# A spectral block with an FFN on one core: the token transform put ahead of the model transform

## The chip, the cores and the metric

The kernel runs on one core of a Trainium2 chip. The core has TensorE (matmuls, PE; its weight loads are PEld), VectorE (DVE), ScalarE (ACT), GpSimd (POOL) and SyncE (SP, which here only issues DMAs), and 16 DMA engines. The metric is the time of one execution on the device, in microseconds; lower is better.

## The reference

x is 2048 tokens by 640 columns in bf16. From a vector c come six rows of 640 columns: mod = silu(c) @ w_mod, named sa, ca, ga, sb, cb, gb. Then:

```
h = layernorm(x) * (1 + ca) + sa
X = rfft2(h) over (tokens, columns)          # 2048 x 321 frequencies
x = x + ga * irfft2(X * (w_r + 1j * w_i))
h = layernorm(x) * (1 + cb) + sb
x = x + gb * ((silu(h @ w_gate) * (h @ w_up)) @ w_down)     # 640 -> 1728 -> 640
```

## The kernel before

Everything is one core's program, written out by hand: each engine runs its instructions in the order of the text, and the tile framework adds semaphores. Every DMA issued by SP stands in one queue in program order, and each also waits for the end of the eighth DMA before it.

**Layout of the tokens.** Partition p of row tile t holds token 16p + t, so there are 16 tiles of 128 x 640. The 640 columns are split as d = 4m + r, plus a last piece of 128 columns, and the 321 column frequencies are built from 81 (l = 0 to 80) by combining the four r.

**The forward stage** goes through the 16 tiles in the order SEQ. For a tile, t1 (L340, L341) transposes its five pieces on TensorE, and ACT copies them to SBUF as hT (L343). The mean and variance come for seven tiles (BN) from bn_stats on DVE (L348, L349), for the others from a Gram product on TensorE (gram_stats, L365) of which DVE sums the diagonal (L367); POOL takes the power -0.5 (L359). dfwd runs the model (column) transform with the table Rs, whose rows carry 1 + ca (dft_d, L320, L323). zout (L387, DVE) takes the mean out and writes Z. POOL scales the token table of this tile by the tile's standard deviation (gscale, L374, L375), and s1 (L398, L399) multiplies it with Z: a complex 128-point token transform, four matmuls of 324 columns. ACT writes the result to A_sb (L402; the last tile by pieces, L405), laid out as frequency l by (tile, re/im, r). The tables of seven tiles are mirror images of others, so those tiles are reversed in the copy of hT.

**The filter.** Wn holds w_i and w_r with a third part for their sum, 256 columns each. Wv holds the same for the mirrored token frequency: a DMA writes the reversed rows to DRAM (flip, L272, on SP; its first row by flip_edge, L266 and L268, on POOL), and another loads them back (L431). wsum (L412) adds w_r and w_i, on DVE or POOL, a range of l at a time.

**The spectral loop.** The 81 values of l are in 21 groups of four (48 to 63 first, then the edges 0 and 80, then 1 to 47, then 64 to 79). A_sb is transposed so that (tile, re/im, r) lies on partitions: the first groups on TensorE (t2_pe, L543, copies at L547 and L549), the rest by four DMA transposes (t2_dma, L524). The constant sa enters at token frequency 0 as a sum SA, added by POOL (L550, L564). Then, for a group: stage_a mixes the 16 tiles and the r by one matmul with KS2 (mix, L572) and DVE multiplies with the filter (prod, L599, twice); stage_b transposes the products back (L606) with a copy on ACT (L609); stage_c applies the inverse mix (L627), and evac writes E (L644; the edges L634 to L636). Since E is complex, rot writes a second, rotated copy (L655, on POOL or DVE). The matmuls with single columns of w_mod (mod_col, L585; mod_cols, L313) and ga (mod_bc, L660) are put in between.

**The inverse and the rest.** For each of 16 tiles s1em and s1er (L676, L685) run the inverse token transform from E with the table Htab, ACT copies (L680), the column transform with RI times ga follows (L1201, L1204), and DVE adds x and sums the row (L1206). From the fourth tile on, the second layernorm (L778 to L814, with a DMA transpose at L806) and the loads of the FFN weights (L751 to L763) run beside it. The FFN (L908, L931, L1018, L1030, L1060) goes in chunks of 2, 4, 4 and 6 tiles. L840 is a DMA that POOL issues to load and add FFN weights; the stores are at L901.

Of the kernel before, what the change touches and what calls it, by code (L numbers as in the profile page):

```python
# [23 lines left out]
NG9 = 9  # L24
BN = (0, 1, 4, 8, 10, 12, 14)
SEQ = (0, 1, 2, 15, 3, 14, 4, 13, 5, 12, 6, 11, 7, 10, 8, 9)
FLIP = (15, 14, 13, 12, 11, 10, 9)
# [8 lines left out]
def gslot(t):  # L36
    return t if t < NG9 else NT - t


def flipped(t):  # L40

    return t in FLIP


def _tables():

# [10 lines left out]
    T["R"] = R.astype(_NPBF)  # L67
    p = np.arange(P, dtype=np.float64)
    G = np.zeros((P, NG9, 2, 128))
    H = np.zeros((128, NT, 2, P))  # L70
    for t in range(NT):
        a = 2.0 * np.pi * ((p[None, :] * (16 * p[:, None] + t)) % S) / S
        if not flipped(t):
            G[:, gslot(t), 0, :] = -np.cos(a)
            G[:, gslot(t), 1, :] = np.sin(a)
        H[:, t, 0, :] = np.cos(a.T)
        H[:, t, 1, :] = np.sin(a.T)
    T["G"] = G.astype(_NPBF)
    T["H"] = H.astype(_NPBF)

    def real2(M):
        return np.array([[M.real, M.imag], [-M.imag, M.real]])

    q = np.arange(16)
    KS2 = np.zeros((16, 2, 4, 3, 2, 16, 2))
    KI = np.zeros((3, 2, 2, 16, 2, 16, 4, 2))
    for m in range(4):
        hl, mm = m // 2, m % 2
        k2 = q if hl == 0 else 15 - q
        F16 = np.exp(-2j * np.pi * np.outer(q, k2) / 16)  # L90
        for r in range(4):
            M = real2(F16 * (-1j) ** (m * r))
            if hl:
                M[:, 1] *= -1
            M = M.transpose(2, 0, 1, 3)
            KS2[:, :, r, 1, hl, :, mm] = M[:, :, 0]
            KS2[:, :, r, 0, hl, :, mm] = -M[:, :, 0] - M[:, :, 1]
            KS2[:, :, r, 2, hl, :, mm] = M[:, :, 1] - M[:, :, 0]
            f = (1.0, 1j ** r, (-1.0) ** r, (-1j) ** r)[m]
            for v in range(3):  # L100
                M = real2(F16.conj().T * f * (np.exp(1j * np.pi * r / 4) if v == 2 else 1.0))
                if hl:
                    M[1] *= -1
                if v >= 1:
                    M[:, 1] *= -1
                KI[v, hl, :, :, mm, :, r, :] = M.transpose(0, 2, 3, 1)
    K = np.zeros((128, 3 * 128 + 192))
    for v in range(3):
        K[:, 128 * v:128 * v + 128] = KI[v].transpose(1, 0, 2, 3, 4, 5, 6).reshape(128, 128)
    K[:, 384:] = KS2.reshape(128, 192)  # L110
    T["K"] = K.astype(_NPBF)
# [45 lines left out]
def adaln_block_kernel(ctx, tc, A_x, A_w_r, A_w_i, B_x, B_w_gate, B_w_up, B_w_down, c, w_mod, out):  # L157
# [3 lines left out]
    G_dram = nc.inline_tensor(T["G"], name="tab_G").ap()  # L161
    H_dram = nc.inline_tensor(T["H"], name="tab_H").ap()
    K_dram = nc.inline_tensor(T["K"], name="tab_K").ap()
    RI_dram = nc.inline_tensor(T["RI"], name="tab_RI").ap()

    x_v = A_x.rearrange("o (p t) d -> p (o t) d", t=NT)
    out_v = out.rearrange("o (p t) d -> p (o t) d", t=NT)
# [16 lines left out]
    KS2 = Ktab[:, 384:576]  # L184
# [10 lines left out]
    ssq = const.tile([P, NT], F32, name="ssq")  # L195
    mv = const.tile([P, NT, 2], F32, name="mv")
    bn6a = const.tile([P, 2, 6], F32, name="bn6a")
    rstd = const.tile([P, NT], F32, name="rstd")
    mhalf = const.tile([P, 6], F32, name="mhalf")
    vtmp = const.tile([P, NT], F32, name="vtmp")  # L200
    sc_f = const.tile([P, NC5], F32, name="sc_f")
# [6 lines left out]
    SAx = gb_bc[:, 0:512].rearrange("p (l k) -> p l k", l=4)  # L208
# [4 lines left out]
    wm_sa = rM.cut(6400, [NC5, D])  # L213
    wm_r = rM.cut(12800, [NC5, 4, D])
    A_sb = rA.cut(0, [NL, NT, 2, 4])
    Wn = rW.cut(0, [3, NT, NW])
    Wv = rW.cut(24576, [3, NT, NW])
    Htab = rH.cut(0, [NT, 2, 128])
    RI = rH.cut(8192, [2, 4, 160])
    o = 0  # L220
    Gtab = rE.cut(o, [NG9, 2, 128]); o += 8192
    Rp = rE.cut(o, [5, RC]); o += 1620
    Rs = rE.cut(o, [2, 4, RC]); o += 2592
    Cb = rE.cut(o, [4, 162], F32); o += 2592
    oHT = o; o += 1300 * 5
    oZ = o; o += 1296 * 4
    oGS = o; o += 768 * 4
    oSQ = o; o += 256

    SL = rY.cut(3072, [5, 2, 128])  # L230
# [13 lines left out]

    nc.scalar.dma_start(c_row[:], c)
    wmca_v = wm_v[:, :, D:2 * D]
    nc.sync.dma_start(x_sb[:, 0:1, :], x_v[:, 0:1, :])
    nc.sync.dma_start(wm_ca[:, 0:3], wmca_v[:, 0:3])
    nc.scalar.dma_start(Rp[:, 4:5], R_dram[:, 4:5])
    nc.sync.dma_start(wm_ca[:, 3:5], wmca_v[:, 3:5])  # L250
    nc.sync.dma_start(Rp[:, 0:4], R_dram[:, 0:4])
    nc.sync.dma_start(x_sb[:, 1:2, :], x_v[:, 1:2, :])
    nc.sync.dma_start(x_sb[:, 2:3, :], x_v[:, 2:3, :])
    nc.sync.dma_start(x_sb[:, 15:16, :], x_v[:, 15:16, :])
    nc.sync.dma_start(Gtab[:, 0:4], G_dram[:, 0:4])
    nc.sync.dma_start(x_sb[:, 3:5, :], x_v[:, 3:5, :])
    nc.sync.dma_start(x_sb[:, 13:15, :], x_v[:, 13:15, :])
    nc.sync.dma_start(x_sb[:, 5:7, :], x_v[:, 5:7, :])
    nc.sync.dma_start(Gtab[:, 4:NG9], G_dram[:, 4:NG9])

    dram = ctx.enter_context(tc.tile_pool(name="dram", bufs=1, space=bass.MemoryType.DRAM))
    Wflip = [dram.tile([P, NT, NW], BF16, name=n) for n in ("wflip_i", "wflip_r")]

    def flip_edge(w, f):
        ncol = w.ap[0][0]
        nc.gpsimd.dma_start(f[0:1, 0:NT - 1, :], bass.AP(tensor=w.tensor, offset=w.offset + P * ncol + 65,  # L266
                                                        ap=[[P * NT * ncol, 1], [P * ncol, NT - 1], [1, NW]]))
        nc.gpsimd.dma_start(f[0:1, NT - 1, :], w[0:1, 65:65 + NW])  # L268

    def flip(w, f):  # L270
        ncol = w.ap[0][0]
        nc.sync.dma_start(f[1:P].rearrange("p k l -> k p l"),  # L272
                          bass.AP(tensor=w.tensor, offset=w.offset + 127 * ncol + 65,
                                  ap=[[P * ncol, NT], [-ncol, P - 1], [1, NW]]))

    nc.sync.dma_start(x_sb[:, 10:13, :], x_v[:, 10:13, :])
    flip(A_w_i, Wflip[0])
    nc.sync.dma_start(x_sb[:, 7:10, :], x_v[:, 7:10, :])
    flip(A_w_r, Wflip[1])
    nc.sync.dma_start(wm_sa[:], wm_v[:, :, 0:D])  # L280
    for i, w in ((0, A_w_i), (2, A_w_r)):
        nc.sync.dma_start(Wn[:, i, :, :], w.rearrange("(k2 k1) l -> k1 k2 l", k1=P)[:, :, 0:NW])
    wm_m = wm_v[:, :, 2 * D:6 * D].rearrange("p k (i d) -> p k i d", i=4)
    nc.sync.dma_start(wm_r[:, :, 0, :], wm_m[:, :, 0, :])
    nc.sync.dma_start(KS2, K_dram[:, 384:576])
# [6 lines left out]
    for i in range(5):  # L292
        nc.vector.memset(rE.cut(oHT + 1300 * i, [NC5, 130])[:, :, 128:129], 1.0)
    nc.gpsimd.memset(identb[:], 0.0)
    nc.gpsimd.affine_select(out=identb[:], in_=identb[:], compare_op=ALU.not_equal, fill=1.0, base=0,
                            pattern=[[-1, 128]], channel_multiplier=1)
    nc.scalar.activation(warm[:], warm[:], ACT.Silu)
# [18 lines left out]
    def dft_d(zps, lhs, R):  # L316
        M = lhs[0].shape[-1]
        for h in range(2):
            o_all = zps[0:M, h, 0:2 * RC]
            nc.tensor.matmul(o_all, lhsT=lhs[4], rhs=R[:, 1, 2 * h:2 * h + 2, :].rearrange("p r n -> p (r n)"),  # L320
                             start=True, stop=False)
            for rr in range(2):
                nc.tensor.matmul(zps[0:M, h, rr * RC:(rr + 1) * RC], lhsT=lhs[2 * h + rr], rhs=R[:, 0, 2 * h + rr, :],  # L323
                                 start=False, stop=(rr == 1))

    def zview(zps, M=P):
        return zps[0:M, :, 0:324]


    if True:  # L330
        t1b, hTs, Zs, Gss = {}, {}, {}, {}

        def zbank(t):
            return banks(2 + 2 * (t % 2), 2, [2, 512])

        def t1(t):
            xt = banks(t % 2, 1, [NC5, 128], BF16)
            xr = x_sb[:, SEQ[t], 0:512].rearrange("p (m r) -> p r m", r=4)
            for r in range(4):
                nc.tensor.transpose(xt[:, r, :], xr[:, r, :], identb[:])  # L340
            nc.tensor.transpose(xt[:, 4, :], x_sb[:, SEQ[t], 512:640], identb[:])  # L341
            hT = rE.cut(oHT + 1300 * (t % 5), [NC5, 130])
            nc.scalar.copy(hT[:, :, 0:128], _rev(xt, 127, [[128, NC5], [-1, 128]]) if flipped(SEQ[t]) else xt)  # L343
            hTs[t] = hT

        def bn(t):
            for k in range(2):
                nc.vector.bn_stats(bn6a[:, k, :], x_sb[:, SEQ[t], 320 * k:320 * k + 320])  # L348
            nc.vector.bn_aggr(mv[:, t, :], bn6a[:])  # L349

        def rstd_of(us):
            bns = [u for u in us if u in BN]
            for u in bns:
                nc.vector.tensor_scalar(vtmp[:, u:u + 1], mv[:, u, 1:2], EPS, float(D), ALU.add, ALU.mult)
            for tt in ([slice(u, u + 1) for u in us if u not in BN] if bns else [slice(us[0], us[-1] + 1)]):
                nc.vector.scalar_tensor_tensor(vtmp[:, tt], mv[:, tt, 0], -float(D), mv[:, tt, 0], ALU.mult, ALU.mult)
                nc.vector.scalar_tensor_tensor(vtmp[:, tt], ssq[:, tt], EPS * D, vtmp[:, tt], ALU.add, ALU.add)
# [113 lines left out]
        for t in range(2, NT + 2):  # L471
            if t == 3:
                s1(1, Zs.pop(1), Gss.pop(1))
            if t + 3 < NT:
                t1(t + 3)
# [863 lines left out]
```

## Time and profile before

| | |
|---|---|
| median of 3 runs | 248.94 us (248.66 to 249.97) |
| the profiled execution, first to last instruction | 248.8 us |
| PE, PEld, DVE, ACT, POOL busy | 241.7, 188.8, 209.7, 167.5, 78.8 us |
| forward stage | 0 to 36.4 us |
| handover through the transposes | 36.4 to 45.8 us |
| spectral loop | 45.8 to 64.0 us |
| inverse | 64.0 to 82.4 us |
| FFN | 82.4 to 248.8 us |
| DMA packets | 46191, 34.74 MB |

The stages are cut at instructions: the first t2_pe starts at 36.48, the products of group 5 at 45.77, the first s1em at 63.98, and the first matmul of the FFN at 82.39. In the profile a line such as L599 is the line of the code; "out<-in" names the tiles that are written and read; "idle before" is the time for which the engine had nothing to do ahead of that group, with what ended it. rX, rM, rA, rE, rW, rH, rL and rY are regions of SBUF that several tiles share over time.

### The profile page before, as it was taken

The page shows a single profiled execution, that of the slowest core. Times are in us where ns is not written, and L with a number is a line of the kernel's source. Part 1 is how long each engine was busy: PE and PEld are TensorE (multiplying, and loading weights), DVE is VectorE, ACT ScalarE, POOL GpSimd, SP SyncE. Part 2 cuts the span into 40 slices and gives each one's busy share as a digit, 9 for nine tenths or more (in the row PEclk, how much of TensorE's full clock was granted, in tenths as well). Part 3 has the DMA queues.
Part 4 walks back from the last instruction along what each step waited for, and adds up shares of the span by engine and source line. Part 5 has one row for each costly group of instructions (what it writes and reads, how often), then busy time and mean ns, then how long its engine had stood idle before and what let it go on. Part 6 is the DMA issues. An engine that isn't in the chain of part 4 may idle for free.

```text
span 248.8 us, 6156 instructions
## 1 busy us (share of the span) xinstructions
PE 241.7 (97%) x2317; PEld 188.8 (76%) x2317; DVE 209.7 (84%) x520; ACT 167.5 (67%) x327; POOL 78.8 (32%) x129
## 2 busy tenths in 40 slices
PE   8999997999999999999999999999999999999994
PEld 3778865899999887788887778888765665656773
DVE  4799997898899998789989986788998788779964
ACT  3778665897989698479774478776247777774220
POOL 8477853996151705002004300000442000004410
PEclk9999999999999999999999999999999999999999
DMA  6999999999999999800004210200511000000111
GB/s 215 391 320 322 247 362 250 158 329 395 326 315 308 324 305 156 174 26 3 0 0 93 68 54 4 54 3 0 108 53 53 3 0 1 1 3 0 53 55 53
DMA packets 46191, 34.74 MB, mean 140 GB/s; under 512 B 21779, under 2 KB 42834, under 8 KB 45778
## 3 DMA queue, kind: packets, MB, share of 16 engines
q1 hardware_dynamic: 44368, 30.00, 43.5%
q0 software_dynamic: 1504, 4.28, 7.3%
q8 instruction: 18, 0.29, 0.5%
q14 instruction: 11, 0.09, 0.2%
q10 hardware_dynamic: 290, 0.08, 0.1%
HBM read 27.05 MB, written 4.72 MB: 128 GB/s over the span
## 4 chain that ended last, share of the span: by engine, by line
PE 86%; DMA 5%; DVE 5%; POOL 2%; issue 1%; ACT 0%; DVEq 0%; POOLq 0%; ACTq 0%
PE psum L1060 36%; PE psum L931 19%; PE psum L1030 5%; PE psum L908 3%; PE psum L606 3%; DMA rW<-rL 3%; DMA rL<-rA 3%; PE psum L572 2%; PE psum L301 2%; PE psum L1018 2%; PE psum L627 2%; DVE rE L387 2%; PE psum L676 1%; PE psum L398 1%; PE psum L323 1%; PE psum L320 1%
## 5 line engine op out<-in xcount | busy, mean ns | idle before, releaser
L1060 PEld LDWEIGHTS <-rW 128*128 128x128 bf16 (+1 forms) x429 | 42.0, 98 | 12.6
L1060 PE MATMUL psum<-rW 128*128 128x256 bf16 (+1 forms) x247 | 42.2, 287 | 0.0
L957 POOL TENSOR_TENSOR rM<-rM,rL 128x320 f32<-128x320 f32 x6 | 5.4, 907 | 96.6 <-ACT rL L956 96.6
L931 PEld LDWEIGHTS <-rE 128*128 128x128 f16 (+1 forms) x196 | 19.0, 97 | 7.8
L599 DVE TENSOR_TENSOR rM<-psum,rW 128x384 bf16<-128x384 f32 (+4 forms) x44 | 20.5, 523 | 3.0 <-PE psum L572 1.7
L931 PE MATMUL psum<-rE 128*128 128x320 f16 (+1 forms) x147 | 22.9, 299 | 0.0
L1098 ACT COPY rX<-psum 128x384 f32<-128x384 f32 (+2 forms) x27 | 14.0, 519 | 7.5 <-PE psum L1060 7.4
L1060 PEld LDWEIGHTS <-rE 128*128 128x128 f16 x156 | 15.3, 98 | 4.7
L1091 ACT COPY rH<-psum 128x384 f32<-128x384 f32 (+2 forms) x27 | 13.9, 516 | 7.2 <-PE psum L1060 5.8
L1095 DVE TENSOR_TENSOR rH<-psum,rM 128x512 bf16<-128x512 f32 (+1 forms) x24 | 15.0, 624 | 4.4 <-PE psum L1060 2.2
L1114 ACT ACTIVATE rL<-psum 128x384 bf16<-128x384 f32 (+2 forms) x27 | 14.4, 532 | 5.3 <-PE psum L1060 3.4
L1099 DVE TENSOR_TENSOR rX<-psum,rX 128x384 f32<-128x384 f32 (+2 forms) x27 | 16.3, 604 | 1.6 <-ACT rX L1098 1.4
L1085 ACT COPY rM<-psum 128x384 f32<-128x384 f32 (+2 forms) x27 | 13.9, 515 | 4.0 <-PE psum L1060 3.9
L1060 PE MATMUL psum<-rE,rY 128*128 128x256 f16 (+1 forms) x78 | 15.6, 290 | 0.0
L1060 PE MATMUL psum<-rW,rE 128*128 128x256 bf16 (+1 forms) x78 | 15.6, 290 | 0.0
L609 ACT CAST rY<-psum 128x512 bf16<-128x512 f32 (+2 forms) x21 | 11.9, 573 | 4.7 <-PE psum L606 4.5
L1115 ACT ACTIVATE rL<-rX 128x384 bf16<-128x384 f32 (+2 forms) x27 | 15.1, 558 | 0.0
L343 ACT COPY rE<-psum 128x640 bf16<-128x640 bf16 x16 | 11.1, 694 | 5.8 <-PE psum L341 4.9
L387 DVE SCALAR_TENSOR_TENSOR rE<-rE,mv,psum 128x648 bf16<-128x648 f32 (+1 forms) x17 | 14.1, 833 | 0.7 <-PE psum L323 0.6
L1206 DVE SCALAR_TENSOR_TENSOR rM<-psum,rX 128x640 f32<-128x640 f32 x16 | 13.0, 820 | 1.7 <-PE psum L1204 1.6
L1030 PE MATMUL psum<-rW 128*128 128x256 bf16 x130 | 14.4, 273 | 0.0
L900 DVE TENSOR_TENSOR rA<-psum,rM 128x320 bf16<-128x320 f32 (+1 forms) x27 | 12.1, 471 | 2.4 <-PE psum L908 2.2
(223 smaller groups left out, 666.8 us busy)
## 6 DMA issues: line engine op xcount, KB each, us to landing
out_dram<-rA SPq DMA_DIRECT2D x31, 80.0 KB, 1.6
rM<-in_w_mod_dram SPq DMA_DIRECT2D x3, 800.0 KB, 10.1
rA<-in_B_w_down_dram SPq DMA_DIRECT2D x2, 960.0 KB, 15.5
rY<-in_B_w_gate_dram POOLq DMA_DIRECT2D x2, 832.0 KB, 8.4
rM<-in_w_mod_dram SPq DMA_DIRECT2D x1, 1600.0 KB, 7.2
rW<-in_B_w_gate_dram SPq DMA_DIRECT2D x2, 640.0 KB, 7.3
rW<-in_B_w_up_dram SPq DMA_DIRECT2D x2, 640.0 KB, 7.9
rW<-in_A_w_i_dram SPq DMA_DIRECT2D x1, 1024.0 KB, 11.0
```

The costliest lines, as they stand in the source:

```text
L387: nc.vector.scalar_tensor_tensor(Zv[:, h], Cv[:, h], mv[:, t, 0:1], zps[:, h], ALU.mult, ALU.subtract)
L599: nc.vector.tensor_tensor(PPs[g][:, v0:v1, hl], xv[:, v0:v1, hl], in1, ALU.mult)
L931: nc.tensor.matmul(o, lhsT=lhs[rows(k), k], rhs=rhs[rows(k), k], start=start and k == ks[0], stop=stop and k == ks[-1], skip_group_check=True)
L1030: nc.tensor.matmul(gu[u], lhsT=Wgu[:, u, c5, ff * 128:(ff + 1) * 128], rhs=h2T[:, :, c5, :], start=(c5 == 0), stop=(c5 == NC5 - 1))
L1060: nc.tensor.matmul(o[:, f], lhsT=w, rhs=b, start=(start and f == 0 and i == 0), stop=(stop and f == len(groups[g]) - 1 and i == len(ops) - ...
L1085: nc.scalar.copy(c0, X)
L1091: nc.scalar.copy(c2, X)
L1095: nc.vector.tensor_tensor(c11, Z, c0, ALU.add)
L1098: nc.scalar.copy(c3, X)
L1099: nc.vector.tensor_tensor(c22, Y, c3, ALU.add)
L1114: nc.scalar.activation(g21, X, ACT.Silu, scale=-1.0)
L1115: nc.scalar.activation(g22, c22, ACT.Silu, scale=-1.0)
```

## The change

The two transforms change places, and the tokens are laid out anew.

- Partition p of a pair t (0 to 7), half h, holds token 1024h + 8p + t. A pair is transformed as one 256-point real transform over (h, p): the table M is 256 columns wide per half. It gives token frequencies 1 to 127 as cosine and sine (partitions 0 to 126 of each of two blocks, ck = 0, 1); partition 127 holds the sums at frequencies 0 and 128, which are real.
- Layernorm is applied to x itself: xhat writes (x - mean) * rstd in bf16, on DVE for tiles 0, 1, 2, 4, 8, 12 and on POOL for the others. Statistics come from bn_stats for 14 tiles and from two ACT passes with an accumulator for tiles 3 and 5. gram_stats, gscale, zout and the transposes t1 go.
- st_a multiplies the normalised tiles (as weights) with M: ten matmuls of 256 columns per pair. ht_ev copies the result, 1280 columns, on ACT. st_b runs the model transform from it, twice six matmuls, and a_ev writes A_sb, on ACT or, for three of sixteen and parts of the last, on DVE.
- The filter is one tile Wt of 16 x 321 columns: rows 0 to 7 loaded straight, rows 8 to 15 the reversed ones. The two flips to DRAM are issued by POOL, of 1024 rows with 642 B each; the loads back by SP. wsum does both ends of the columns in two operations per half.
- The frequencies of partition 127 (16 of them, at multiples of 128) have their own mix and filter. They run as a side chain (sp_...) through spare PSUM columns in the loop, and come back through DRAM into partition 127 of E.
- E now carries both parts from stage_c (Em is 2 x 32 x 128): rot goes. The table H is loaded for half of the tiles (512 KB instead of 1024) and POOL writes the other half with a sign. RI times ga moves from DVE to POOL.
- The edges 0 and 80 accumulate into one column of group 5's bank. SA is not added to the transposed tiles any more, only to the special row.
- Order of the loads on SP: three pairs of x and the first part of M ahead of w_mod and R; H ahead of the last parts of w_mod; the four transfers of the special row ahead of the down weights.

The diff, cut to its core:

```diff
-            nc.sync.dma_start(f[1:P].rearrange("p k l -> k p l"),
...
+        nc.gpsimd.dma_start(f[:].rearrange("p k l -> k p l"),
+                            bass.AP(tensor=w.tensor, offset=w.offset + 255 * 321, ap=[[256 * 321, 8], [-321, P], [1, 321]]))
...
+        def st_a(t):
+            xh = xhs[t % 3]
             for c5 in range(NC5):
+                for h in range(2):
+                    lhsT = xh[:, h, 512:640] if c5 == 4 else xh[:, h, 0:512].rearrange("p (m r) -> p r m", r=4)[:, c5, :]
+                    nc.tensor.matmul(zA[:, c5], lhsT=lhsT, rhs=Mtab[:, t, h], start=(h == 0), stop=(h == 1))
+        def ht_ev(t, lo=0, hi=NC5, eng=None):
+            (eng or nc.scalar.copy)(HTs[t % 3][:, lo:hi], zA[:, lo:hi])
+        def st_b(t, ck):
+            zps = banks(4 + 2 * ck, 2, [4, 256])
+            lhs = [HTs[t % 3][:, c5, 128 * ck:128 * ck + 128] for c5 in range(NC5)]
...
+        for t in range(8):
+            if t + 1 < 8:
+                st_a(t + 1)
+                ht_ev(t + 1, 0, 3 if t == 6 else NC5)
+                if t == 6:
+                    ht_ev(7, 3, 5, nc.vector.tensor_copy)
+            u = 2 * t + 6
             if u < NT:
+                bn(u)
+            if u - 2 < NT:
+                xpair(u - 2)
+            if u < NT:
+                bn(u + 1)
+                rstd_of(u, 2)
...
+            for ck in range(2):
+                st_b(t, ck)
...
+                elif (t, ck) in on_dve:
+                    a_ev(t, ck, eng=nc.vector.tensor_copy)
+                else:
+                    a_ev(t, ck)
...
+        def sp_sums():
+            sps = psum[:, 3, 128:128 + NL]
+            for i in range(10):
+                r, c2 = i // 2, i % 2
+                nc.tensor.matmul(sps, lhsT=SL[:, r, c2, :], rhs=Rp[:, 8 if r == 4 else r, 81 * c2:81 * c2 + 81], start=(i == 0), stop=(i == 9))
+            nc.vector.tensor_scalar_mul(SA[:], sps, 256.0)
...
+            elif i == 2:
+                for h in range(2):
+                    nc.scalar.copy(Osp[:, 40 * h:40 * h + 40], gap(128, h, 40, b))
+                nc.sync.dma_start(Esc[0][:], Osp[:, 0:64])
+                nc.sync.dma_start(Esc[1][:], Osp[:, 64:80])
+                nc.sync.dma_start(Em[127:128].rearrange("p v q c -> p (v q c)"), Esc[0][:].rearrange("(o p) n -> o (p n)", o=1))
+                nc.sync.dma_start(Er[127:128].rearrange("p v q c j -> p (v q c j)"), Esc[1][:].rearrange("(o p) n -> o (p n)", o=1))
...
+        SPG = (10, 12, 14)
...
         for g in range(NG + 1):
-            if g > 1:
-                sa_add(g + 4)
...
+            for lo, rk in {1: ((16, 0), (16, 8)), 4: ((32, 0), (32, 8)), 8: ((64, 0), (64, 8))}.get(g, ()):
+                wsum(lo, lo + 16, rk, nc.gpsimd)
+            if g == 1:
+                sp_sa()
+            if g == 3:
+                sp_sums()
+                sp_w(1)
...
+            if g == 7:
+                sp_gather()
             if 0 < g < NG - 2:
+                if g in SPG:
+                    sp_mm(SPG.index(g), g)
                 stage_a(g + 2)
+                if g in SPG:
+                    sp_ev(SPG.index(g), g)
```

## The prediction

> **What bounds it now.** I read the busy table first, then the chain of waits in order of time, the timeline around its seams, and the busy time by stage.
>
> ```profile
> PE 241.7 (97%) x2317; PEld 188.8 (76%) x2317; DVE 209.7 (84%) x520; ACT 167.5 (67%) x327; POOL 78.8 (32%) x129
> DMA  6999999999999999800004210200511000000111
> ```
>
> TensorE is busy nearly throughout, and the 16 DMA engines are full in the first 16 of 40 slices (6.2 us each): up to about 99 us a step also depends on what its data queue behind. By stage, columns as PE, PEld, DVE, ACT, POOL, clock, DMA share, GB/s:
>
> ```profile
> 0.00:36.40 36.40, 35.02 (x375) 25.79 (x375) 29.89 (x110) 24.19 (x39) 26.64 (x58) 1.00 0.98 308
> 36.40:45.80 9.40, 7.44 (x94) 5.99 (x94) 6.53 (x18) 6.07 (x12) 4.48 (x10) 1.00 1.10 251
> 45.80:64.00 18.20, 18.08 (x336) 17.83 (x334) 16.85 (x37) 15.87 (x26) 13.61 (x23) 1.00 1.10 313
> 64.00:82.40 18.40, 18.20 (x259) 16.50 (x257) 16.34 (x47) 16.52 (x34) 7.06 (x13) 1.00 1.11 315
> ```
>
> The forward transform is TensorE's (35.0 of 36.4). The second stage, the handover through the transposes, has 2 us of TensorE idle. The spectral loop has PE, DVE and ACT all at 87% or more: little can be added to any of them. From 64 us on the arithmetic is not changed. The chain crosses the handover like this (start, length, what):
>
> ```profile
> 36.48 0.30 PE psum L543 x4
> 36.79 6.61 DMA rL<-rA
> 43.47 0.26 POOL rL L564
> 43.73 1.08 POOL rW L412
> 44.83 0.48 DVE rM L599
> 45.35 0.49 PE psum L572 x4
> ```
>
> At 36.79 the DMA transposes start; L564 and L412 (a filter sum on POOL) then hold the products (L599) until 44.83.
>
> **The forward transform.** Durations are from these groups (busy, mean ns of one):
>
> ```profile
> L387 DVE SCALAR_TENSOR_TENSOR rE<-rE,mv,psum 128x648 bf16<-128x648 f32 x15 | 13.1, 871 | 0.6 <-PE psum L323 0.6
> L402 ACT CAST rA<-psum 128x648 bf16<-128x648 f32 x15 | 10.5, 700 | 3.6 <-PE psum L399 3.1
> L374 POOL TENSOR_SCALAR rE<-rE,rstd 128x256 bf16<-128x256 bf16 x16 | 7.9, 491 | 3.6 <-DMA rE<-tab_G 2.2
> L348 DVE BATCH_NORM_STATS2 bn6a<-rX 128x6 f32<-128x320 bf16 x14 | 6.2, 482 | 0.0
> L644 ACT CAST rE<-psum 128x1024 bf16<-128x1024 f32 x7 | 7.1, 1019 | 0.0
> ```
>
> TensorE: the 128x162 matmuls come 0.07 us apart (two in 0.14 in the chain), so 2.4 columns per ns. A tile now takes 640 transposed columns, 645 of the Gram product (9 of 16 tiles), 1296 and 1296: in all 57,500, or 24.0 us. Afterwards a pair takes 10x256 + 2x1296 = 5152, eight of them 41,200, or 17.2 us: 2.15 us per pair. ACT: the 640-element copies (0.694) go; a pair costs one 1280-element copy (1.24 us, from L644 at 512 and 1024 elements: 0.585, 1.019) and two of 648 (L402, 0.70): 2.64 us.
>
> DVE: L387 and the Gram reductions go, but nearly every tile now has its statistics here: two L348 and one aggregate (0.209), 1.12 us a tile as in the timeline (8.12 to 9.24). 14 of 16 tiles: 15.7 us, against 7 tiles now. Six normalised tiles on DVE at 0.39 (L443 and L444: 0.304 for 324 elements, 0.258 for 162): 2.3. Small ones, the same lines' kind (eight variances, seven means, Rs): 4.3. One eviction ahead of the last pair's mean: 0.83 (L639 and the DVE form of L644, 0.684 for 512, 1.216 for 1024). Sum 23.1 us. Two pairs need more from POOL (two tiles at 0.95, from L374, L375 and L814, and a power at 0.70), which is about DVE's 2.6 per pair. **So DVE becomes the bound of this stage**, 2.6 to 2.95 us per pair, above ACT's 2.64 and PE's 2.15.
>
> Start: the first pair (320 KB, twice what came before) lands at about 4.0; now DVE takes its first tile at 3.67. The R table is the eighth load, 2.6 MB in; at 215 GB/s in the first slice and 391 in the second that is 9.4 us, before DVE wants it (10.9). 4.0 + 23.1 + 1.3 of waits for POOL (next paragraph) = 28.4. Tail: two tiles on POOL 1.9, one TensorE stage 1.1, its eviction 0.9, two halves of the model transform 1.1, evictions by pieces 0.3 and then about 1.0. Columns 48 to 63 are there at 33.7, all at 34.5. The first transpose on TensorE moves from 36.48 to **33.7**, the DMA transposes from 36.79 to 34.4.
>
> The filter's flip moves from SP (0.69 and 1.53 us of issue) to POOL, with 1024 runs each. The nearest rows: POOL's issue takes 0.51 us for one run and 1.02 for 256 (L840, mean of two), so 2.55 us by the slope; the bounds are 0.51 and 4 x 1.02 = 4.1. Behind each flip stand a power and a tile that DVE's next mean waits for: at 2.55 DVE waits 1.3 us in all, and each further microsecond costs about 2.2, as the two are in series. [...]
>
> **The handover.** Now products 0 to 3 wait for the second flip to land (0.73 us on DVE) and for L412 (0.77). Afterwards the filter is 2.6 MB of loads instead of 4.2, the flips are 1.3 instead of 2.1 MB, and 10.7 MB stand ahead of the transposes instead of 12.25, which took until 40.8; at that rate they end at 35.6, so the transposes land at about 40 and are hidden. DVE from 34.7: filter sums 0.58, products 0 to 2 3.3 (L599, 0.55 each), sums 0.58, products 3 and 4 2.0, to 41.4. But the sums for the shift now stand on PE ahead of group 5: they wait for POOL's copies (0.31 + 0.76 + 0.76 after a cast at 39.4) until 41.3, then ten matmuls 0.55 and group 5's mix. Group 5's products start at 42.5; now at 45.77 (44.83 and two of 0.47). **-3.3 us.**
>
> **The loop.** Same mixes, products and inverse columns. Added: three products 81x64 on DVE (0.75), four copies on ACT (1.0, less L634's 0.38), eleven small matmuls (0.6); two rotations on DVE go (0.5). Three engines nearly full: +0.6, between 0 and 1.2. The columns of w_mod that L585 reads (now landing at about 56.7, used at 57.16) stand behind H afterwards (+1.4 us) and behind transposes that are 2.4 to 3.7 us earlier: they land at 54.3 to 55.6, wanted at 54.4; +0.5, between 0 and 1.8.
>
> **The special row** goes out to DRAM and comes back to partition 127, two transfers in series. The first is issued at about 54.3, behind w_mod and RI, and lands near 59; the second, on an empty queue, takes about 2 (stores at the end: 1.6), so 61.6 to 62, when the inverse starts at 61.8. Cost 0, bounds 0 and 9.7 (rival below). The down weights stand behind it on SP, issued at 60 instead of 51.8; 3 MB to the first gate columns at 0.35 MB/us are there at 70, used at 80. L655's rotations after the loop go: -0.3, between -0.9 and 0.
>
> **Sum**: -3.3 + 0.6 + 0.5 - 0.3 = -2.5 of the span, 248.8 to 246.3. The FFN keeps its length. The median of the runs (248.94) is 0.1 above this span: **246.4 us**.
>
> **Rivals.**
> 1. *Better*: DVE's tiles overlap more than I think and ACT's 2.64 sets the pace: eight pairs, 21 us after 10.9, end the stage 2.6 us earlier; 243.8. For: DVE was gap-free at 1.12. Against: the order of its queue, which holds the next mean behind each power.
> 2. *No gain*: the flips take 4.1 us on POOL, so DVE waits 3.4 more and the stage ends as late as now: 249.8, or about 248.9 at 3.7. For: 1024 runs; against: 256 cost only 0.5 above one. [...]
> 3. *Slower*: the special row is late. If each of its two transfers takes what small ones took in busy time (4.5 to 4.9 us for the flips' edges, 8.2 for the 40 KB of down weights), the inverse starts at 64.5 to 71.5, that is 249.1 to 256. It decides from 4.6 us a transfer on. For: 128 B and 32 B runs, one partition at the end, SP blocked between. Against: the queue is empty by then.
>
> Chances: forecast 0.50, rival 1 0.15, rival 2 0.15, rival 3 0.20. Of them faster by over 0.5% 0.64 (0.5% is about what a measurement of this kernel can tell from no change), within 0.14, slower 0.22. The range leaves out a tenth each side: 242.5 to 251.5.
>
> **What would show it.** The first transposes on TensorE near 33.7 and DVE without gaps from 4 to 28 (step one); POOL's two flips at 2 to 3 us; group 5's products at 42.5 behind a TensorE wait for POOL; the loop 18.8 us long; the inverse's first matmul released by something other than the load of partition 127. Wrong if DVE sits idle behind POOL or a load in the forward stage, if the inverse waits for the special row, or if the FFN's first gate waits for weights.

## The result, and the profile after

The changed kernel takes **261.93 us** (median of 4 runs, 259.72 to 264.62), the kernel before 248.88 us beside it: ratio 1.048, 95% interval 1.042 to 1.054. It is slower, where the forecast was 246.4 us in a range of 242.5 to 251.5. The profiled execution is the longest of the four (264.62 us, span 262.8), 2.7 us above the median; the stage that went wrong first looks the same, within 1 us, in a second run that shares it (row_q below). Ratios leave slow executions out, so some differ from what the medians say, most of all that of flip_sp_row_q below.

The busy row, TensorE's granted clock and the DMA engines, in 40 slices of 6.6 us:

```profile
PE 239.8 (91%) x2216; PEld 186.5 (71%) x2216; DVE 205.4 (78%) x491; ACT 167.1 (64%) x329; POOL 70.8 (27%) x102
PEclk9797799999999979999999999999999999999999
DMA  6999972999499999970000511020521000000021
```

TensorE has less to do than before (239.8 against 241.7 us) and yet the span is 14.0 us longer: the kernel waits. TensorE's clock falls in several early slices, and the DMA engines, full for 16 slices before, have holes in slices 7 and 11 (a 2 and a 4). Busy time by stage, cut at the first t2_pe, the products of group 5, the first s1em and the first L1041, a matmul of the FFN (L1030 in the kernel before; columns as PE, PEld, DVE, ACT, POOL, clock, DMA share, GB/s):

```profile
0.00:43.00 43.00, 28.52 (x217) 19.89 (x218) 25.95 (x85) 22.57 (x35) 23.98 (x37) 0.88 0.85 251
43.00:52.80 9.80, 8.14 (x122) 7.04 (x123) 6.99 (x20) 5.81 (x12) 1.05 (x4) 1.00 0.98 173
52.80:73.00 20.20, 19.89 (x366) 19.42 (x364) 17.75 (x40) 17.04 (x30) 12.13 (x23) 1.00 0.82 236
73.00:96.20 23.20, 19.93 (x265) 17.57 (x263) 15.53 (x43) 16.94 (x35) 8.22 (x14) 0.97 1.13 266
```

In the first stage no engine is busy for more than 28.5 of 43 us: even the busiest stands idle for a third of it, at 251 GB/s. The fourth has TensorE idle for 3.3 us. The chain of waits names both places (start, length, what):

```profile
4.29 7.80 DMA rE<-tab_R
...
18.75 5.61 issue
24.36 1.74 POOL rE L347 x2
...
82.05 10.34 DMA rW<-rL
```

"issue" at 18.75 hides what POOL waited for, so the timelines of POOL and DVE are read beside it:

```profile
7.35 1.33 POOL L275 DMA_DIRECT2D wflip_i<-in_A_w_i_dram  x1
11.81 1.18 POOL L275 DMA_DIRECT2D wflip_r<-in_A_w_r_dram  x1
24.36 1.73 POOL L347 TENSOR_SCALAR rE<-rX,rstd,nmean 128x640 bf16<-128x640 bf16 x2 [6.81 <-issue]
```

```profile
23.04 0.89 DVE L320 BATCH_NORM_STATS2 bn6a<-rX 128x6 f32<-128x320 bf16 x2 [6.27 <-DMA rX<-in_A_x_dram]
```

DVE stands for 6.27 us until a tile of x lands; POOL, whose next tile needs DVE's mean, stands with it. The table of DMA issues (KB each, median us from issue to landing) says how late x is. The kernel before, 0 to 36 us, and the changed one, 0 to 40 us:

```profile
rX<-in_A_x_dram SPq DMA_DIRECT2D x3, 320.0 KB, 4.9
```

```profile
rX<-in_A_x_dram SPq DMA_DIRECT2D x8, 320.0 KB, 11.7
wflip_i<-in_A_w_i_dram POOLq DMA_DIRECT2D x1, 642.0 KB, 14.9
wflip_r<-in_A_w_r_dram POOLq DMA_DIRECT2D x1, 642.0 KB, 13.9
```

x takes 11.7 us, 15.4 and 16.1 for its last two pairs, against 4.7 to 6.1 before, while the two turns of the filter (the flips, which reverse its rows), issued at 7.35 and 11.81, are under way beside it for 14 to 15 us. Not all of the difference is theirs: in the new order the eight loads take 8.0 us without any turn (median, flip_none below).

At the second place SP's timeline carries it:

```profile
56.30 0.98 SPq L482 DMA_DIRECT2D rH<-tab_RI  x1
65.51 0.33 SPq L655 DMA_DIRECT2D esc<-rE  x1
...
68.49 1.71 SPq L762 DMA_DIRECT2D rA<-in_B_w_down_dram  x2
```

SP stands for 8.2 us until ACT has the special row, and the down weights behind it are issued at 68.5 instead of 51.8. They and the gate weights are still moving when the transposes of the second layernorm come at 82.05; these take 10.34 us where they took 6.61.

### The profile page after: what moved, and what is told of

Its sections match the earlier page's. It is cut to its first block, busy times and chain, and to the rows that moved or that the text cites. A ratio compares the mean times of both kernels' runs of the same rounds, so it can differ in the third digit from the quotient of the medians.

```text
span 262.8 us, 5888 instructions
## 1 busy us (share of the span) xinstructions
PE 239.8 (91%) x2216; PEld 186.5 (71%) x2216; DVE 205.4 (78%) x491; ACT 167.1 (64%) x329; POOL 70.8 (27%) x102
## 4 chain that ended last, share of the span: by engine, by line
PE 77%; DMA 7%; DVE 5%; issue 4%; ACT 3%; POOL 2%; SPq 1%; DVEq 0%; ACTq 0%; POOLq 0%
PE psum L1071 34%; PE psum L942 17%; PE psum L1041 6%; DMA rW<-rL 4%; PE psum L356 3%; DMA rE<-tab_R 3%; PE psum L919 3%; PE psum L540 2%; DVE rM L533 2%; PE psum L509 2%; ACT rE L359 2%; PE psum L1029 2%; PE psum L679 2%; PE psum L565 2%; POOL rE L347 1%
## 5 line engine op out<-in xcount | busy, mean ns | idle before, releaser
L942 PEld LDWEIGHTS <-rE 128*128 128x128 f16 (+1 forms) x196 | 18.9, 97 | 8.1 <-DVE rE L896 0.4
L356 PE MATMUL psum<-rE 128*128 128x256 bf16 x80 | 12.5, 307 | 12.3 <-POOL rE L347 8.3
L533 DVE TENSOR_TENSOR rM<-psum,rW 128x384 bf16<-128x384 f32 (+2 forms) x42 | 20.3, 543 | 3.3 <-PE psum L509 2.4
L320 DVE BATCH_NORM_STATS2 bn6a<-rX 128x6 f32<-128x320 bf16 x28 | 12.3, 479 | 9.7 <-DMA rX<-in_A_x_dram 9.7
L356 PEld LDWEIGHTS <-rE 128*128 128x128 bf16 x80 | 8.8, 118 | 15.5 <-POOL rE L347 10.1
L359 ACT CAST rE<-psum 128x1280 bf16<-128x1280 f32 (+1 forms) x8 | 9.4, 1172 | 13.3 <-PE psum L356 13.3
L1041 PE MATMUL psum<-rW 128*128 128x256 bf16 x130 | 15.4, 284 | 0.0
## 6 DMA issues: line engine op xcount, KB each, us to landing
rX<-in_A_x_dram SPq DMA_DIRECT2D x8, 320.0 KB, 11.7
```

What stands on the lines that cost most here:

```text
L356: nc.tensor.matmul(zA[:, c5], lhsT=lhsT, rhs=Mtab[:, t, h], start=(h == 0), stop=(h == 1))
L359: (eng or nc.scalar.copy)(HTs[t % 3][:, lo:hi], zA[:, lo:hi])
L533: nc.vector.tensor_tensor(PPs[g][:, v0:v1, hl], xv[:, v0:v1, hl], in1, ALU.mult)
L942: nc.tensor.matmul(o, lhsT=lhs[rows(k), k], rhs=rhs[rows(k), k], start=start and k == ks[0], stop=stop and k == ks[-1], skip_group_check=True)
L1041: nc.tensor.matmul(gu[u], lhsT=Wgu[:, u, c5, ff * 128:(ff + 1) * 128], rhs=h2T[:, :, c5, :], start=(c5 == 0), stop=(c5 == NC5 - 1))
```

## The experiments

All times are first starts in the profiled execution, in us. "Ratio" is to the kernel before, with its 95% interval.

| run | median | ratio | t2_pe | group 5 | s1em | L1041 | span |
|---|---|---|---|---|---|---|---|
| before | 248.9 to 249.6 | | 36.4 | 45.2 | 64.0 | 83.2 | 248.8 |
| changed | 261.93 | 1.048 (1.042 to 1.054) | 43.0 | 52.7 | 72.9 | 96.2 | 262.8 |
| flip_sp | 258.33 | 1.034 (1.028 to 1.040) | 34.5 | 48.4 | 68.5 | 89.3 | 255.5 |
| flip_none | 253.23 | 1.014 (1.008 to 1.020) | 34.7 | 44.3 | 64.5 | 86.2 | 251.8 |
| row_q | 261.25 | 1.048 (1.041 to 1.055) | 42.0 | 51.7 | 74.5 | 93.4 | 259.1 |
| flip_sp_row_q | 259.13 | 1.026 (1.018 to 1.035) | 34.3 | 48.9 | 73.5 | 94.1 | 259.5 |
| no_row | 249.46 | 0.999 (0.997 to 1.002) | 34.9 | 44.6 | 63.7 | 82.7 | 248.2 |
| row_direct | 263.90 | 1.058 (1.052 to 1.063) | 34.3 | 45.3 | 77.6 | 96.5 | 261.8 |
| ga_sums | 257.20 | 1.031 (1.026 to 1.035) | 34.0 | 45.4 | 67.0 | 89.2 | 255.4 |
| all4 | 261.27 | 1.049 (1.042 to 1.055) | 35.3 | 44.1 | 74.2 | 93.2 | 258.6 |
| before_pool | 255.13 | 1.024 (1.021 to 1.028) | 42.3 | 49.4 | 68.5 | 87.5 | 252.9 |
| before_none | 248.64 | 0.996 (0.995 to 0.998) | 36.2 | 43.3 | 62.3 | 81.2 | 246.8 |
| flip_order | 258.73 | 1.036 (1.031 to 1.041) | 36.0 | 51.0 | 71.2 | 92.1 | 257.8 |
| none_row_pool | 250.62 | 1.005 (1.003 to 1.007) | 34.5 | 44.2 | 64.3 | 83.6 | 249.1 |

In the kernel before, group 5 starts at 45.22 by its trace. The 45.77 used further up adds two products of 0.47 us to 44.83, but the product at 44.83 is the last of the edges, and group 5 follows it at once.

**flip_sp: the turns behind x, on SP's queue.**

```diff
-        nc.gpsimd.dma_start(f[:].rearrange("p k l -> k p l"),
+        nc.sync.dma_start(f[:].rearrange("p k l -> k p l"),
...
     load_x(4, 4)
+    flip(A_w_i, Wflip[0])
+    flip(A_w_r, Wflip[1])
```

> The two turns of the filter are issued on SP's queue behind the last pair of x instead of on POOL's queue; all else as in the changed kernel (262.8 us span in its profile, t2_pe at 43.0). Theory A (turns in a queue of their own take the DMA engines' time from the x pairs that stand in SP's queue): the last x lands at about 15 instead of 22 to 26 us, VectorE's 6.3 us wait for x and POOL's 6.8 us go, the first transposes on TensorE come at 36 to 37, the run is 255 to 257 us. Rival B (there is too much to load ahead of x, whatever the queue): x still lands past 20 us, transposes at 41 to 43, 260 or more. Rival C (the turned half, now last, is late for the products): transposes at 36, but the first product waits for the filter's load.

Measured 258.33 us. x lands in 6.7 us, POOL's and DVE's long waits are gone, and the first transposes come at 34.5: for the stage theory A, and even better than it expected. The run misses its 255 to 257: only 3.6 of the 8.5 us arrive at the end. Behind the turns the first columns of w_mod for ga are now late; from the chain of waits:

```profile
30.81 10.26 DMA rM<-in_w_mod_dram
41.11 1.94 PE psum L663 x10
```

TensorE waits for them until 41.1, and holds the products of group 5 until 48.4. The edit changes the queue of the turns and also when they start. No run keeps them on POOL's queue and holds them back until x has landed, so these two are not told apart.

**flip_none: no turn at all.**

```diff
-            nc.sync.dma_start(Wt[:, 2 * i, 8:16, :], Wflip[i][:])
+            nc.sync.dma_start(Wt[:, 2 * i, 8:16, :], bass.AP(... offset + 321, ap=[[321, P], [256 * 321, 8], [1, 321]]))
```

> Leaves the turn of the filter out: the second half of the filter is loaded straight from its rows, in their order (so the products use a filter that is not reversed). Theory A: the same stage times as with the turns on SP, 255 to 257 us, since the turns' bytes then stand behind x in both; rival D (the turns' own bytes and short runs cost the stage even behind x): at least 2 us faster than the turns on SP.

Measured 253.23 us, 5.1 less than with the turns on SP: rival D. The turn is not only in the way by its place. From 16 to 24 us (windows as above, PE, PEld, DVE, ACT, POOL, clock, DMA share, GB/s), with the turns on SP:

```profile
16.00:20.00 4.00, 3.25 (x30) 2.66 (x29) 3.56 (x15) 2.43 (x3) 3.09 (x4) 1.00 0.73 201
20.00:24.00 4.00, 3.75 (x38) 3.23 (x37) 3.83 (x15) 3.31 (x4) 2.77 (x4) 1.00 0.63 125
```

and without them:

```profile
16.00:20.00 4.00, 3.25 (x31) 2.64 (x29) 3.60 (x13) 2.43 (x3) 3.15 (x5) 1.00 1.14 323
20.00:24.00 4.00, 3.64 (x36) 3.04 (x34) 3.83 (x14) 3.57 (x5) 2.98 (x4) 1.00 1.11 312
```

The engines compute alike; the DMA engines move 163 GB/s instead of 318 on average and are not even full (shares of 0.73 and 0.63 against 1.14 and 1.11), while SP stands 5.4 us in the issue of the second turn and 5.0 in that of the load behind it. Eight microseconds at 155 GB/s less are 1.2 MB, which all that stands behind gets later.

**before_pool: this one part in the kernel before.**

```diff
-        nc.sync.dma_start(f[1:P].rearrange("p k l -> k p l"),
+        nc.gpsimd.dma_start(f[1:P].rearrange("p k l -> k p l"),
```

> The kernel before with one part of the change alone: its two turns (1 MB read and written, each) are issued on POOL's queue instead of SP's, where they stood behind most of x. Theory A (a queue of its own gives the turn a share of the 16 DMA engines while x is still coming): tiles of x land several us later than their 4.7 to 6.1 us of before, TensorE waits in the forward stage, and the run is 252 to 257 us. Rival (the kernel before takes x in small pieces and early, or TensorE's work hides it): 248.5 to 250.

Measured 255.13 us, 5.7 slower: theory A in the other kernel too. Its x takes 8.2, 8.6 and 11.7 us to land (medians of the loads of 160, 480 and 320 KB; 4.7, 6.1 and 4.9 before), and the first transposes move from 36.4 to 42.3. POOL issues these turns at 1.25 and 2.55, earlier than the changed kernel does, and they are larger (1016 KB each instead of 642).

**before_none: what the turn cost before.** The edit is that of flip_none, in the kernel before (flip and flip_edge go).

> The kernel before without the turn (the second half of the filter is loaded from its rows in their order, so it is not reversed). Theory L (its forward stage is bound by TensorE, 35.0 of 36.4 us, and the turn is hidden beside it): only the waits of 0.7 and 0.8 us for the turned half go, 247.8 to 249.0. Rival M (the turn costs the kernel before as much as the changed one, where it was worth 5 us on SP's queue): 243.5 to 245.

Measured 248.64 us against 249.40 in the same session: theory L, 0.8 us. With TensorE busy for 35.0 of 36.4 us, one turn issued behind 13 of the 16 tiles of x and the other behind all of them, the turn was hidden. In the changed kernel a turn on SP's queue does not lengthen the stage either (34.5 with it, 34.7 without); what it delays there is the loads behind it, which the handover wants 2 us earlier than before.

**flip_order: the loads in the order of the kernel before.** Turns at the last two pairs of x; w_mod's columns for sa and ga ahead of the turned halves.

```diff
-    load_x(4, 4)
+    load_x(4, 2)
+    flip(A_w_i, Wflip[0])
+    load_x(6, 2)
+    flip(A_w_r, Wflip[1])
+    nc.sync.dma_start(wm_sa[:], wm_v[:, :, 0:D])
     load_w(0, A_w_i)
     load_w(2, A_w_r)
+    nc.sync.dma_start(wm_r[:, :, 0, :], wm_v[:, :, 2 * D:3 * D])
```

> The turns on SP's queue as in the run with 258.3 us, but in the order of the kernel before: one turn ahead of the last two pairs of x, one behind, then the columns of w_mod for the shift and the gate (1.6 MB), the unturned halves, and the turned halves last. Theory N (part of the 5.1 us that the turn still costs on SP's queue is the order, since SP stood 5 us in the issue of the second turn and L663 waited until 41.1 for w_mod): L663 no longer waits, 255 to 256.5. Rival O (all of it is wanted by 37 us, so that another load is late in place of w_mod): 257.5 to 259, with the products waiting for the filter.

Measured 258.73 us: rival O. The matmuls on w_mod (L664 here) no longer wait for a load, but what is put last is late in its place; DVE's waits now name the turned half:

```profile
DVE rW L381 <- DMA rW<-wflip_r: 3.8, 1, 3.8
```

**ga_sums: the matmuls that wait for loads moved back.**

```diff
-        ga_mod(320, 5)
-        ga_mod(0, 0)
...
+            if g == 2:
+                ga_mod(320, 6)
+                ga_mod(0, 7)
+                sp_sums()
+                sp_w(1)
```

> The turns on SP (258.3 us alone); and the two matmul chains on w_mod's first columns (L663), and the sums for the shift with the row's filter transposes (L611), are issued on TensorE in iteration 2 of the loop instead of ahead of it and in iteration 3, into the two banks that are free there. Theory J (TensorE's in-order queue held the products of groups 3 to 5 behind a load that lands at 41.1): group 5's products move from about 48.5 to 45 or 46, the first inverse matmul from 68.7 to 65.5 to 66.5, the run 255 to 256.5. Rival K (the filter's turned half, or DVE's own work, holds the products anyway): less than 1 us gained.

Measured 257.20 us. Group 5 moves by the 3.0 us of theory J (48.4 to 45.4), but the inverse by 1.5 and the run by 1.1, which its interval does not tell from nothing: the gather of the special row then waits for the fourth DMA transpose, TensorE for the gather (1.3 us at 52), and the transposes of the second layernorm still take 9.2 us. Most of the gain was given back at the next waits.

**row_q: the special row off SP.** Stores on ACT's queue, loads on POOL's.

```diff
-                nc.sync.dma_start(Esc[0][:], Osp[:, 0:64])
+                nc.scalar.dma_start(Esc[0][:], Osp[:, 0:64])
...
-                nc.sync.dma_start(Em[127:128]...
+                nc.gpsimd.dma_start(Em[127:128]...
```

> The special row's two stores go out on ACT's queue and its two loads on POOL's, so that SP, which waited 8.2 us for them, issues the down and gate weights at 57 instead of 68.5 us; all else as in the changed kernel. Theory E (the late weights share the engines with the transposes of the second normalisation, which took 10.3 us instead of 6.6, and leave TensorE idle there): the transposes take 6 to 7 us, the run is 257 to 259. Rival F (the transposes are slow, or TensorE idle there, for another reason): 261 to 262. Rival G (the row itself is then late, behind 5 MB of weights): TensorE waits for the row at the inverse, 263 or more.

Measured 261.25 us, no gain, and yet both E and G are seen. The weights are issued at 56.9, and from the first s1em to L1041 it takes 18.9 us instead of 23.3 (E). But the row, now behind the weights, takes 5.3 us out and 4.1 back, and the inverse waits for it (G); from the chain of waits:

```profile
70.31 4.08 DMA rE<-esc
```

**flip_sp_row_q: both edits together.**

> Both edits together. If the two losses are independent, their gains add: 262 less 6 less 4, about 251 to 253 us; if the second loss only follows from the first (all behind it shifted), no better than the turns on SP alone, 255 to 257. Under 248 would mean that the changed kernel's order was faster but for these two.

Its ratio, 1.026, makes about 256 us, and even the lower end of its interval (1.018) makes 254: the gains do not add. The interval (1.018 to 1.035) overlaps that of flip_sp, so whether the second edit adds anything stays open here. The inverse is again released by the row's load (5.40 us), at 73.5.

**row_direct: one transfer from SBUF to SBUF, on ACT's queue,** with the turns on SP.

```diff
+                nc.scalar.dma_start(Em[127:128].rearrange("p v q c -> p (v q c)").rearrange("o (p n) -> o p n", n=64), Osp[:, 0:64])
+                nc.scalar.dma_start(Er[127:128].rearrange("p v q c j -> p (v q c j)").rearrange("o (p n) -> o p n", n=16), Osp[:, 64:80])
```

> The turns on SP (258.3 us alone), and the special row carried to partition 127 by one transfer from SBUF to SBUF on ACT's queue for each of the two tiles, in place of a store to DRAM and a load behind it. With two in series behind the weights (5.6 and 5.4 us) the inverse started at 73.5 instead of 68.7. Theory E/G (SP must not be blocked, and the row must not stand through two transfers in series): one transfer takes 5 to 6 us and lands before the loop's end, the inverse starts at 68.5 to 69.5 with no wait for it, the transposes of the second normalisation take 6.5 to 7.5 us, the run 255.5 to 257. Rival: the single transfer with its 128 B runs to one partition takes 9 us or more behind the weights, the inverse waits as long as with two, 259 or more.

Measured 263.90 us: neither. The transfer itself takes 6.3 us, near the 5 to 6 expected, but ACT's timeline shows a wait that the theory had not:

```profile
58.47 0.54 ACTq L655 DMA_DIRECT2D rE<-rE  x1
67.45 0.48 ACTq L656 DMA_DIRECT2D rE<-rE  x1
67.97 0.58 ACT L543 CAST rY<-psum 128x512 bf16<-128x512 f32 x1 [9.53 <-DMA rA<-in_B_w_down_dram]
```

The second issue comes 0.02 us after a load of down weights on SP's queue (15.91 us from 51.52) has landed (67.43). In the kernel before, SP's L256 waits 0.5 us for a load that ACT issued (tab_R, at 1.29, with 3.8 us to landing; L256 starts at 5.09). So in these two the program's wait of a DMA for an earlier one goes over both queues; and ACT, which evicts the loop, stands in it for 9.5 us, TensorE with it.

**all4: row_direct, ga_sums, and the row's evictions behind stage_b's copy.**

> The turns on SP, the row by one transfer on ACT's queue, the chains and the sums late, and the row's evictions behind the eviction of the group's own second stage: if the gains add, 258.3 less 2 less 2.5 less 0.5 to 1 gives 252.5 to 254; if one loss only takes the place of another, 255 to 257. Under 248.8 is not expected: without the turn at all the changed order gave 253.2.

Measured 261.27 us, above both; the chain goes through the row's first transfer (6.19 us), for which ACT's second issue waits here, and ACT behind it. In both runs the loss is ACT standing in an issue, for the down weights in the one and for the row itself in the other.

**none_row_pool: the same single transfer on POOL's queue,** without the turn.

> Leaves the turn out as the run with 253.2 us, and carries the special row by one transfer from SBUF to SBUF for each tile on POOL's queue, so that neither SP nor ACT stands for it. Theory E (the row costs 3.8 us because SP stands behind its store and the weights come late, not by its matmuls): 250 to 251, with the transposes of the second normalisation at 6 to 7 us and the inverse starting at 64.5 to 65. Rival (a row under load is late on any queue): the first inverse matmul waits for it, 252.5 or more.

Measured 250.62 us: theory E. SP does not stand, nobody waits for the row (6.4 us from 57.2, the loop ends at 64.3), and the transposes of the second layernorm take 6.4 us where those of flip_none take 8.0 (medians of four).

**no_row: no turn, and nothing of the row but its sums and its filter,** which stay on TensorE.

> Leaves out the turn of the filter, as the run without it (253.2 us, group 5's products at 44.3, first inverse matmul at 64.7), and beyond that the whole special row: its gather, its matmuls and evictions in the loop, its stores and loads (so partition 127 of E carries no frequency). Theory H (the row's small operations cost the loop 1.5 to 2.2 us beyond what was forecast, and its stores and loads, by blocking SP, 2.5 us at the second normalisation): first inverse matmul at 62.5 to 63.2, the transposes of the second normalisation 6 to 7 instead of 9.3 us, the run 248 to 249.5. Rival I (the loop is longer for another reason, the loads or TensorE): first inverse matmul at 64 or later, and only the transposes gain, 250.5 to 252.

Measured 249.46 us, what the kernel before takes. Of theory H the second half holds in full and the first in part: the row's operations cost the loop 0.8 us (64.5 to 63.7), and its blocking of SP 2.8 (from s1em to L1041, 21.7 to 18.9).

**What follows.** By the ratios, the loss of the changed kernel against the one before is the turn beside x on a queue of its own (1.048 to 1.034, about 3.4 us), the turn's transfers behind x (1.034 to 1.014, about 5.0) and the special row (1.014 to 0.999, about 3.6). By the intervals each part is good to some 2 us, and they are parts in this order of edits only: on the changed kernel itself, row_q gained nothing. What is left of the change is worth nothing: 0.999 (0.997 to 1.002), and the kernel before, with its turn left out too, stands at 0.996 (before_none). No run here beats the kernel before with all of its work done. A turn made on chip was not tried, and why the DMA engines move so little beside the turn (163 GB/s; its runs are of 642 B, with DRAM on both sides) is not shown.

## Why the prediction was wrong, point by point

The span was to be 246.3 and is 262.8 in the profiled run, the longest. Its 16.5 us of error lie so: first t2_pe at 43.0 instead of 33.7 (9.3), handover 9.7 instead of 8.8 (0.9), loop 20.2 instead of 19.3 (0.9), from s1em to L1041 23.3 instead of 18.9 (4.4), and the rest 166.6 instead of 165.6 (1.0).

- **The step that failed is "The forward transform", in its sum "4.0 + 23.1 + 1.3".** It takes every later pair of x to be there when it is wanted. The flips' move was priced as POOL's issue alone, 2.55 us each; the issue took 1.33 and 1.18, and what cost was the transfer, which left SP's queue and so came in beside x. "10.7 MB ... at that rate" used the rate of before for a traffic in which the turns ran at half of it. Without the turn the step holds within 1.2 us (34.5 to 34.9), but in part by luck. DVE, named as the bound, has done its statistics at 27.7 in flip_none (28.4 forecast), and the chain of waits runs elsewhere:

```profile
20.24 1.24 ACT rE L359
21.52 1.27 PE psum L356 x10
```

  st_a and the copy behind it wait for each other, since zA is one buffer; the next copy starts at 22.86, so 2.62 us a pair. The forecast had counted the two apart, and had 2.6 to 2.95 for DVE.
- **The R table** landed at 12.1, not 9.4. It landed at 11.8 without the turn too (flip_none), so this miss is not the turn's.
- **The handover's gain of 3.3 us** was counted from 45.77. From the 45.22 of the trace it is 2.7, all of it from the earlier first transposes, and the handover itself was to stay at 8.8 us. Where the turn is gone it takes 9.7 and group 5 starts at 44.2 to 44.6, a gain of 0.6 to 1.0. The wait for POOL's copies was there as said; TensorE's matmuls on w_mod's columns ahead of it (1.52 and 0.77 us in flip_none) were not counted.
- **The loop** at "+0.6" and "+0.5": from 45.22 it took 18.8 us before and takes 20.2 now, so 1.4 stands against the forecast 1.1. The rest of the 0.9 is the start that was misread.
- **"The special row ... Cost 0"** was right for the inverse, whose first matmul waited for the loop, and wrong for SP. The down weights were to be issued at 60, with the row's first store at 54.3; ACT had the row at 65.5. That the transposes run beside late weights (10.34 us for the first; the median of four is 6.4 in none_row_pool) was in no step. (The 4.4 us are the profiled run's; the four other runs that keep the row on SP take 20.7 to 22.2 from s1em to L1041, 1.8 to 3.3 above the forecast.) Rival 3 (two transfers in series, late) is what row_q shows, at 5.3 and 4.1 us.
- **"The FFN keeps its length"**: 1.0 us more. An estimate from the granted clock, 0.50 from the first L1041 at 96.2 to 98.3, gives the same: half of 2.1 us.
- Rivals 1 and 2 had only issue times and engines in them. The flip at 7.35 ran beside DVE's L345 and took 1.33 us to issue, against 1.30 in before_pool with DVE idle (there for 1016 KB). What got longer was DVE's work: L345 took 0.85 us beside this flip and L411 0.85 beside the one at 11.81; without flips they take 0.43 (the mean of six) and 0.30 (flip_none, where L411 is L409). They ended at 8.80 and 13.03, just behind the issues (8.68 and 12.98).

What bears on the failed step is the landing time of x once another queue has work, which no step of the forecast had. In before_pool it is 8.2, 8.6 and 11.7 us against 4.7, 6.1 and 4.9 before, in the changed kernel 11.7 us against 8.0 in flip_none (medians). How the DMA engines share their time between two queues was not shown.

## What to carry to other kernels

The flips that moved to another engine were not paid by their issue (1.33 and 1.18 us): in SP's queue they stood behind the loads that are wanted first; on POOL's they ran beside them, and x landed in 11.7 us instead of 8.0. So price a moved transfer by what it now runs beside, and give each load a time by which it must land. And ask of each wait on an issuing engine what stands behind it: SP's 7 us for a row of 20 KB (flip_none) cost 2.8 us at a transpose some 15 us later, and a wait in ACT's queue stopped the loop for 9.5 us.

## What the runs showed of the hardware

TensorE's granted clock fell to 0.50 around three waits of the changed kernel, and came back to 1.00 some 4 us after the work did. TensorE's last matmul before the 6.6 us of waiting ends at 18.75; the granted clock is 1.00 until 22, 0.80 from 22 to 24, 0.50 from 24 to 30, then 1.00. The first matmuls of a pair before, in and after that stretch (TensorE's timeline; in the middle one, the tenth matmul had run alone at 25.29):

```profile
16.33 1.28 PE L356 MATMUL psum<-rE 128*128 128x256 bf16 x10 [1.32 <-POOL rE L347]
...
26.14 2.11 PE L356 MATMUL psum<-rE 128*128 128x256 bf16 x9 [0.45 <-POOL rE L347]
...
30.12 1.25 PE L356 MATMUL psum<-rE 128*128 128x256 bf16 x10
```

The pair took 3.98 us (26.14 to 30.12) instead of 2.42, so this wait cost 1.6 us beyond its length. By the granted clock in windows of 0.25 and 0.5 us, the three falls of this run are (us; "stops" is the end of the last matmul before the wait, "resumes" the start of the matmuls that follow each other closely again):

| stops | clock falls to 0.50 | resumes | clock back at 1.00 |
|---|---|---|---|
| 6.25 | 9.5 | 8.9 | 12.9 |
| 18.75 | 23.2 | 26.1 | 30.0 |
| 90.7 | 94.9 | 94.8 | 98.3 |

So it fell 3.3 to 4.4 us after the last matmul, and was back 3.5 to 4.0 us after the close work began. The third is behind the late transposes, with three single matmuls in its wait.
